# A transformer block in fp32: another order of the seven second products, two more steps in the second norm, a split of the row maxima on other engines, and a second store buffer

## The chip, the cores and the metric

The kernel runs on one core of a Trainium2 chip. A core has five engines that work side by side, each through its own instructions in order: TensorE (PE, matrix products; PEld is its weight load), VectorE (DVE), ScalarE (ACT), GpSimd (POOL) and SyncE (SP), which issues the DMAs here. They wait for each other by semaphores. The metric is device time in microseconds (us): the kernel before took 2392.91 us as the median of three runs (2387.88 to 2393.16).

## The reference

One transformer block on 2048 tokens of width 576, conditioned by a vector `c`:

```
mod = (silu(c) @ w_mod).reshape(c.shape[0], 6, 1, -1)
sa, ca, ga, sb, cb, gb = (mod[:, i] for i in range(6))
h = layernorm(x) * (1 + ca) + sa
x = x + ga * attention(h)           # 32 heads of width 18, one key and one value head for all
h = layernorm(x) * (1 + cb) + sb
x = x + gb * mlp(h)                 # layernorm again, 576 -> 4608, gelu (tanh form), 4608 -> 576
```

Scores of the attention are scaled by 18 ** -0.5 and go through a softmax over 2048 keys. All inputs and outputs are fp32.

## The kernel before, in words

**Split numbers.** Products of the large operands run in a format of fewer bits (F32R). An operand is therefore split into a high part (rounded by a copy into F32R) and a low part (the value minus the high part), and a product is three matmuls: high by high, high by low, low by high. Most of POOL's work, and some of ACT's and DVE's, is making such pairs.

**Stages.** A short stage makes the modulation, the first norm and the queries, keys and values. Then comes the attention, then the MLP, in two halves of 1024 tokens each.

**Attention.** 32 quads of four heads and 512 tokens (`NQT`), each with 16 steps `kc` of 128 keys. ACT takes the exponentials of the scores (L796). At the same time PE and DVE work on the next quad: for each query the maximum of its scores is found by L315 (products), L816 and L814 (reductions on DVE). `smax_fin2` (L351) closes this at `kc` 13: PE transposes the 16 columns of maxima, ACT copies the negative to `mf` (L356), POOL makes the high part `ms[:, 0]` (L357) and the low part (L358), and four DMAs (L362) write these rows into the next quad's operand `qst`; the scores of the next quad need them. Two lists are worked off beside that, in `between` (L818), a step at a time: `fill` (one step in every second `kc`) and `prep` (one step in most `kc`).

`fill` holds, from quad 8 on, the output projection of a finished block (`wo_block`) and then `ln2_block` (L566): the norms ahead of the MLP, tile by tile (`ln2_tile`, L519). For blocks 0 and 1 (`fine`) such a tile is: statistics of X in two steps (DVE bn_stats L140 and L144, then POOL L146 and L147); three POOL operations that make `h` (L536 to L538); one step later bn_stats of `h` on DVE (L140 again); and so on to the transposes. Eight such tiles fall into the attention, four from quad 8 and four from quad 16 on; the other eight (blocks 2 and 3) lie in the MLP's first half.

`prep` is `weight_parts` (L657): POOL multiplies the second MLP weight, forms sums of its quarters, splits each (L664 high, L665 low, into a buffer named `r2`) and SP stores it to DRAM (`w2scr`, `w2sum`, and for some groups of the first weight `w1scr`). There is one `r2` buffer, so a split waits until the store of the one ahead has left it.

**MLP.** 18 groups of 256 hidden columns (`NG`), for each of the two token halves: 36 steps `v`. The first product of a step is done in Strassen's way, in seven products (`product`, L1010, names A11, S2, S3, A12, S1, A22, S4, in this order, 6 or 8 matmuls of 512 columns each) on sums of quarters of the tokens that `op_pieces` (L877) makes. `gelu` (L1015) follows in three parts that are issued by calls of `g_()`: ACT (bias, square), then DVE and tanh on ACT, then the last product on DVE (L1032) with the split of the result into a unit (ACT L1034 high, POOL L1035 low).

The second product of a step `v` is issued in pieces of 12 matmuls of 288 columns by calls of `t_()`, one between each two products of step `v` + 1. In the first half it is plain (`fc2`, L1128). In the second half (`v` of 18 to 34) it is again seven products (`fc2s`, L1085), in the order of the table `SEVEN`: the operands are four quarters of the gelu's result (A11, A12, A22 are split as they are) and four sums (S1 to S4) that `sums` (L1062) makes on POOL (L1072 to L1082, with L1069 and L1070 for the split), issued step by step by calls of `s_()`. From the second such step on, the last of the seven pieces comes a step later, so that what PE runs in step `v` + 1 is: product A11, piece 7 of the step before; product S2, piece 1; product S3, piece 2; product A12, piece 3; product S1, piece 4; product A22, piece 5; product S4, piece 6. Gelu A12 of step `v` is the last to start, at product S4, and its third part is issued after product S2 of step `v` + 1. The pieces are gathered in two PSUM buffers (`psA`) and added to the result by DVE (L1103). Their seven weight buffers `W2S` are loaded anew from `w2scr` and `w2sum` by `load_w2s` (L1055) as soon as a piece is done.

## Time and profile before

| | |
|---|---|
| median of three runs | 2392.91 us |
| the profiled execution's own time | 2392.28 us |
| its span, first to last instruction | 2390.5 us |
| mean granted TensorE clock | 0.986 of full |
| PE busy | 2313.4 us (97%) |
| DVE busy | 1882.9 us (79%) |
| ACT busy | 1656.6 us (69%) |
| POOL busy | 1296.0 us (54%) |
| attention, roughly | 140 to 1450 us |
| MLP, first and second half, roughly | 1466 to 1930, 1930 to 2390 us |

A busy PE in this table is one with a matmul in flight, not one at its peak. In rows of the timeline the columns are start, duration of the group, engine, line, operation, tiles, shape and count, and in brackets the idle time of the engine before the row and what ended it. In rows of stretches the columns are the stretch, its length, the busy time of PE, PEld, DVE, ACT and POOL with their numbers of instructions, the granted clock, the DMA share and GB/s.

### The profile page before, as it was taken

Reading aid. Unit: us, or ns where it says so; the run is one execution under the profiler, and the core shown is the slowest. Engines: PE = TensorE matmul, PEld = TensorE weight load, DVE = VectorE, ACT = ScalarE, POOL = GpSimd, SP = SyncE. Lnnn points to the kernel's source line nnn. Section 1 sums busy time; section 2 is a strip of 40 time slices with the busy share of each in tenths; the row PEclk is TensorE's granted clock in tenths of the full one; section 3 lists DMA queues with packets and bytes.
Section 4 is the critical chain, followed back from the end, with each engine's and each line's share of the span. In section 5 each row is a group of like instructions: output and inputs, shape, how many; then the busy total and the mean of one; then the engine's idle time right before and its main releaser. Section 6 shows DMA issues by size and latency. Waiting matters only on the chain.

```text
span 2390.5 us, 44703 instructions
## 1 busy us (share of the span) xinstructions
PE 2313.4 (97%) x16382; PEld 1432.6 (60%) x16382; DVE 1882.9 (79%) x3330; ACT 1656.6 (69%) x3163; POOL 1296.0 (54%) x1552
## 2 busy tenths in 40 slices
PE   8999999999999999999999999999999999999998
PEld 6643444454434443434544336999999888888877
DVE  6589999979989879989799955666666767767766
ACT  5569999979989878989799996444444534333333
POOL 6501444436664346564434332688888656666666
PEclk9999999999999999999999999999999999999999
DMA  6412122221222112222122224334444465555553
GB/s 217 139 60 71 49 80 79 78 69 66 69 68 75 66 58 80 70 70 72 67 68 81 72 70 148 131 139 169 157 154 167 147 183 160 163 153 160 160 157 110
DMA packets 145627, 259.92 MB, mean 109 GB/s; under 512 B 15755, under 2 KB 56587, under 8 KB 145409
## 3 DMA queue, kind: packets, MB, share of 16 engines
q1 hardware_dynamic: 145409, 257.07, 33.7%
q8 instruction: 129, 2.11, 0.4%
q14 instruction: 89, 0.73, 0.1%
HBM read 156.11 MB, written 92.01 MB: 104 GB/s over the span
## 4 chain that ended last, share of the span: by engine, by line
PE 81%; POOL 6%; ACT 4%; DMA 3%; DVE 3%; issue 2%; SPq 1%; POOLq 0%; DVEq 0%; ACTq 0%
PE psC L783 19%; PE psB L1010 16%; PE psA L1128 9%; PE psB L794 9%; PE psM L315 9%; PE psA L1097 8%; PE psB L804 4%; PE psB L244 2%; ACT P L796 2%; PE psB L595 2%; POOL big L1035 1%; DMA w2scr<-r 1%; ACT big L1034 1%; DMA w2sum<-r 1%; POOL Z L536 1%
## 5 line engine op out<-in xcount | busy, mean ns | idle before, releaser
L796 ACT ACTIVATE P<-psB 128x512 f32<-128x512 f32 x2048 | 1049.9, 619 | 19.9 <-PE psB L794 17.2
L816 DVE TENSOR_REDUCE mx<-psM 128x1 f32<-128x512 f32 x1476 | 944.9, 683 | 61.2 <-PE psM L315 28.7
L783 PE MATMUL psC<-P,V 128*32 128x256 f32 (+1 forms) x6056 | 603.9, 470 | 12.6 <-ACT O L614 12.6
L315 PE MATMUL psM<-KS,qst 64*128 64x512 f32 x1722 | 600.0, 435 | 10.8 <-DVE mx L816 10.8
L794 PE MATMUL psB<-qst,KS 64*128 64x512 f32 x2048 | 602.9, 436 | 4.5 <-DMA qst<-ms 3.0
L794 PEld LDWEIGHTS psB<-qst,KS 64*128 64x128 f32 x2048 | 302.1, 185 | 173.2 <-issue 75.7
L1010 PE MATMUL psB<-ops,w1a 128*128 128x512 f32 x1512 | 400.9, 403 | 3.2 <-DVE gx L1032 2.5
L315 PEld LDWEIGHTS psM<-KS,qst 64*128 64x128 f32 x1722 | 286.8, 186 | 134.4 <-DVE mx L814 93.2
L1010 PEld LDWEIGHTS psB<-ops,w1a 128*128 128x128 f32 x1512 | 278.6, 193 | 53.6 <-DVE gx L1032 3.4
L783 PEld LDWEIGHTS psC<-P,V 128*32 128x32 f32 x6056 | 119.9, 108 | 235.8 <-issue 212.3
L1128 PE MATMUL psA<-w2s,big 128*128 128x288 f32 x1488 | 256.2, 296 | 0.0
L1128 PEld LDWEIGHTS psA<-w2s,big 128*128 128x128 f32 x1488 | 221.7, 188 | 6.7 <-POOL big L1035 0.2
L807 ACT ACTIVATE xc<-psB 128x512 f32<-128x512 f32 x246 | 148.8, 605 | 92.8 <-PE psM L315 71.4
L1103 DVE TENSOR_TENSOR XT<-psA,XT 128x576 f32<-128x576 f32 x170 | 125.2, 753 | 87.0 <-PE psA L1097 85.5
L1030 ACT ACTIVATE psB<-gs 128x512 f32<-128x512 f32 x144 | 86.7, 602 | 122.5 <-DVE gs L1029 122.5
L814 DVE CUSTOM_DVE_ANT_0 xc<-psM,xc 128x512 f32<-128x512 f32 x246 | 167.4, 680 | 3.3 <-PE psM L315 2.3
L1097 PE MATMUL psA<-w2s,big 128*128 128x288 f32 x816 | 131.2, 309 | 26.0 <-POOL big L1035 13.8
L1132 DVE TENSOR_TENSOR XT<-psA,XT 128x576 f32<-128x576 f32 x152 | 113.1, 748 | 47.3 <-PE psA L1128 47.1
L1097 PEld LDWEIGHTS psA<-w2s,big 128*128 128x128 f32 x816 | 119.9, 196 | 42.1 <-ACT big L1034 19.6
L1035 POOL TENSOR_TENSOR big<-gx,big 128x512 fp32r<-128x512 f32 x72 | 97.5, 1354 | 86.9 <-ACT big L1034 86.5
L804 PEld LDWEIGHTS psB<-KD,qst 64*128 64x128 f32 x246 | 45.3, 184 | 163.7 <-ACT P L796 112.6
L1034 ACT ACTIVATE big<-gx 128x512 fp32r<-128x512 f32 x72 | 45.6, 633 | 126.5 <-DVE gx L1032 126.5
(196 smaller groups left out, 3278.8 us busy)
## 6 DMA issues: line engine op xcount, KB each, us to landing
w1a<-w1scr SPq DMA_DIRECT2D x154, 256.0 KB
w1scr<-w1a SPq DMA_DIRECT2D x98, 256.0 KB
w2scr<-r SPq DMA_DIRECT2D x72, 288.0 KB
w2sum<-r SPq DMA_DIRECT2D x68, 288.0 KB
w2s<-w2sum SPq DMA_DIRECT2D x68, 288.0 KB
w2s<-w2scr SPq DMA_DIRECT2D x29, 576.0 KB
qst<-qscr SPq DMA_DIRECT2D x192, 72.0 KB
w2s<-w2scr SPq DMA_DIRECT2D x34, 288.0 KB
```

The costliest lines, as they stand in the source:

```text
L315: pe.matmul(o, QST[n][64 * g:64 * g + 64, p, 128 * qt:128 * (qt + 1)], KS[64 * g:64 * g + 64, 512 * kb:512 * (kb + 1)], start=True, stop=True)
L783: pe.matmul(PVt[n][32 * j:32 * (j + 1), cs], V[:, kc, :], t[:, j, cs], start=(kc == 0 and h0 == 0), stop=(kc == 15), skip_group_check=True)
L794: pe.matmul(t, KS[64 * g:64 * g + 64, 128 * kc:128 * (kc + 1)], QST[n][64 * g:64 * g + 64, i, :], start=True, stop=True)
L796: ac.activation(P[n, kc][:, 2 * i + g, :], t, AF.Exp, scale=SCALE)
L804: pe.matmul(t, QST[n][64 * g:64 * g + 64, p, 128 * qt:128 * (qt + 1)], KD1[64 * g:64 * g + 64, :], start=True, stop=True)
L807: ac.activation(XC[-1], t, AF.Relu)
L814: ve.tensor_tensor_reduce(c, t, c, 1.0, -3.0e38, ALU.add, ALU.max, o)
L816: ve.tensor_reduce(o, t, axis=AX.X, op=ALU.max)
L1010: pe.matmul(o, x, y, start=(first and i == 0), stop=(i == len(terms) - 1), skip_group_check=True)
L1097: pe.matmul(p[:, i, :288], x[:, ts_], W2S[k][:, y], start=(bool(first) and q == 0), stop=(q == 2), skip_group_check=True)
L1103: ve.tensor_tensor(o, p[:, :, :288], o, op=ALU.add)
L1128: pe.matmul(p[:, nn, :288], x, y, start=(q == 0), stop=(q == len(terms) - 1))
```

## The change

Five edits, which shift the lines below them by one or two:

1. The table `SEVEN` lists the pieces as S3, A22, A11, A12, S2, S1, S4 (before: A11, A12, S3, A22, S2, S1, S4), and `load_w2s` loads the weights in the same order. `sums` has one step less (S2's split goes with the two sums ahead of it), and its later steps are issued after products A11, S3 and A12 (before: after S2, S3, A12 and S1).
2. `ln2_tile` for blocks 0 and 1 has two steps more between `h` and its statistics.
3. `smax_fin2`: ACT writes the high part of the maxima straight from PSUM, DVE makes the low part from PSUM; POOL has no part in it any more; `ms` has one buffer, `mf` is gone.
4. `r2`, the buffer of the split weights ahead of their store, has two buffers and lies in another pool; `bst` has three buffers instead of four.
5. In `op_pieces` the low part of T4 goes to the engine `e2`, and for step 0 `e2` is POOL: POOL makes the low parts of T4 and B22 there, and of T4 at step 18.

```diff
     def smax_fin2(n):
         p = psB()
         pe.transpose(p[:16, :128], MR.pop(n), ident)
-        ms = pa.tile([16, 2, 128], F32R, name="ms", bufs=2)
-        mf = pa.tile([16, 128], F32, name="mf", bufs=2)
-        ac.activation(mf, p[:16, :128], AF.Copy, scale=-1.0)
-        po.tensor_copy(ms[:, 0], mf)
-        po.tensor_tensor(ms[:, 1], mf, ms[:, 0].bitcast(F32), op=ALU.subtract)
+        ms = pa.tile([16, 2, 128], F32R, name="ms")
+        ac.activation(ms[:, 0], p[:16, :128], AF.Copy, scale=-1.0)
+        ve.scalar_tensor_tensor(ms[:, 1], p[:16, :128], -1.0, ms[:, 0].bitcast(F32), op0=ALU.mult, op1=ALU.subtract)
...
         po.tensor_tensor(h, h, BC[:, 0, :], op=ALU.add)
         yield
-        if not fine:
+        yield
+        if fine:
             yield
         mv, rs = small()
         stt = ln_stats1(h)
...
-            o = px.tile(shape, F32R, name="r2")
+            o = pb.tile(shape, F32R, name="r2", bufs=2)
...
-              "T3": (10, 0, ve), "T4": (12, 2, ve), "t0": (0, 4, e2), "t1": (1, 9, e2)}
+              "T3": (10, 0, ve), "T4": (12, 2, e2), "t0": (0, 4, e2), "t1": (1, 9, e2)}
...
-    SEVEN = (("A11", 1, None), ("A12", 0, (0, 0)), ("S3", 1, (1, 1)), ("A22", 0, (1, 0)), ("S2", 1, None),
+    SEVEN = (("S3", 1, (1, 1)), ("A22", 0, (1, 0)), ("A11", 1, None), ("A12", 0, (0, 0)), ("S2", 1, None),
              ("S1", 1, (1, 1)), ("S4", 0, (0, 1)))
...
-        w = ("B11", "B21", "T3", "T4", "T2", "T1", "B22")[k]
+        w = ("T3", "T4", "B11", "B21", "T2", "T1", "B22")[k]
...
         po.tensor_tensor(s2, s1, h[0][0], op=ALU.subtract)
-        yield
         parts("S2", s2)
...
+    form = op_pieces(YR[0], po)
     b2_scaled(B2["b"])
...
         w_("A11")
         ac.activation(U[:, 0], ba, AF.Copy)
         g_()
+        s_()
...
         if v != 1:
             t_()
         g_()
-        s_()
         more("-B11 +T2", "-T4")
...
         gens.append(gelu(v, 1, 1, be))
         g_()
-        s_()
         more("-T3 -B21")
```

The places where instructions move. First PE in the middle of the MLP's second half, before: from product A11 of a step to its product A12 and the piece behind it. L1010 is a product, L1097 a piece of the second product; `big` holds the units of A12 and the sums, `gt` those of A11 and A22, and `w1a` the weight of piece 7.

```order
L1010 MATMUL psB<-ops,w1a 128x512 x6
L1097 MATMUL psA<-w1a,big 128x288 x12
L1010 MATMUL psB<-ops,w1a 128x512 x6
L1097 MATMUL psA<-w2s,gt_24668 128x288 x12
L1010 MATMUL psB<-ops,w1a 128x512 x6
L1097 MATMUL psA<-w2s,big 128x288 x12
L1010 MATMUL psB<-ops,w1a 128x512 x6
L1010 MATMUL psB<-opt,w1a 128x512 x2
L1097 MATMUL psA<-w2s,big 128x288 x12
```

And the same stretch of the changed kernel, where L1009 and L1095 are the same two lines:

```order
L1009 MATMUL psB<-ops,w1a 128x512 x6
L1095 MATMUL psA<-w1a,big 128x288 x12
L1009 MATMUL psB<-ops,w1a 128x512 x6
L1095 MATMUL psA<-w2s,big 128x288 x12
L1009 MATMUL psB<-ops,w1a 128x512 x6
L1095 MATMUL psA<-w2s,gt_24604 128x288 x12
L1009 MATMUL psB<-ops,w1a 128x512 x6
L1009 MATMUL psB<-opt,w1a 128x512 x2
L1095 MATMUL psA<-w2s,gt_24604 128x288 x12
```

Before, the piece behind product S2 reads A11 and the next one A12; now they are S3 and A22, then A11, and A12 comes one product later, behind S1.

POOL in the same part of the program, before, from the sum S3 at the end of a step to the split of S2 in the next. L1072 is S3, L1075 and L1076 are the two other sums, L1069 and L1070 a split, and L1035 the low part of A12:

```order
L1072 TENSOR_TENSOR yr<-yr 128x512
L1069 CAST big<-yr 128x512
L1070 TENSOR_TENSOR big<-yr,big 128x512
L1035 TENSOR_TENSOR big<-yr,big 128x512
L1075 TENSOR_TENSOR yr<-yr 128x512
L1076 TENSOR_TENSOR yr<-yr 128x512
L1069 CAST big<-yr 128x512
L1070 TENSOR_TENSOR big<-yr,big 128x512
```

The changed kernel there (each line number is one less):

```order
L1071 TENSOR_TENSOR yr<-yr 128x512
L1068 CAST big<-yr 128x512
L1069 TENSOR_TENSOR big<-yr,big 128x512
L1074 TENSOR_TENSOR yr<-yr 128x512
L1075 TENSOR_TENSOR yr<-yr 128x512
L1068 CAST big<-yr 128x512
L1069 TENSOR_TENSOR big<-yr,big 128x512
L1034 TENSOR_TENSOR big<-yr,big 128x512
```

S3 has kept its place; the low part of A12 now stands behind the two sums and the split of S2, four operations later.

DVE in the attention, in a quad without norm tiles, before; L348 and L349 close the maxima of a quad and the rows of L816 and L814 are the reductions of the quad after:

```order
L348 TENSOR_REDUCE mxf<-mx_4581 128x8
L349 TENSOR_REDUCE mxf<-mx_4581 128x8
L816 TENSOR_REDUCE mx_5158<-psM 128x1 x5
L814 ISA xc,mx_5158<-psM,xc 128x512
L814 ISA mx_5158 128x1
```

And in the changed kernel:

```order
L348 TENSOR_REDUCE mxf<-mx_4569 128x8
L349 TENSOR_REDUCE mxf<-mx_4569 128x8
L815 TENSOR_REDUCE mx_5144<-psM 128x1 x3
L356 SCALAR_TENSOR_TENSOR ms<-psB,ms 16x128
L815 TENSOR_REDUCE mx_5144<-psM 128x1 x2
L813 ISA xc,mx_5144<-psM,xc 128x512
L813 ISA mx_5144 128x1
```

The low part of the maxima now stands in DVE's order between the third and the fourth of these reductions.

## The prediction

> **What bounds the kernel now.** I read the page first, then the busy times by stretch, then the timeline where a stretch is slow. The span, and the two halves of the MLP by stretch:

> ```profile
> span 2390.5 us, 44703 instructions
> 1938.44:2353.07 414.63, 390.30 (x2145) 338.27 (x2145) 294.46 (x432) 154.22 (x256) 263.63 (x241) 0.96 0.56 158
> 1510.68:1854.00 343.32, 343.32 (x2066) 310.72 (x2065) 224.69 (x363) 155.30 (x271) 291.34 (x390) 1.00 0.45 157
> ```

> In the first half (second row) PE is busy for 343.32 of 343.32 us at a granted clock of 1.00: nothing to win there. In the second half it is busy for 390.30 of 414.63 at 0.96, so PE stands and is also clocked lower. One step of it, in the timeline:

> ```profile
> 2008.49 1.57 PE L1010 MATMUL psB<-ops,w1a 128*128 128x512 f32 x6
> 2009.90 1.75 PE L1097 MATMUL psA<-w2s,gt 128*128 128x288 f32 x12
> 2011.48 1.56 PE L1010 MATMUL psB<-ops,w1a 128*128 128x512 f32 x6
> 2012.36 0.68 DVE L1032 SCALAR_TENSOR_TENSOR yr<-psB,yr 128x512 f32<-128x512 f32 x1
> 2013.76 0.53 PE L1097 MATMUL psA<-w2s,big 128*128 128x288 f32 x2 [0.71 <-ACT big L1034]
> 2013.78 1.27 POOL L1035 TENSOR_TENSOR big<-yr,big 128x512 fp32r<-128x512 f32 x1 [4.21 <-ACT big L1034]
> 2015.10 2.55 PE L1097 MATMUL psA<-w2s,big 128*128 128x288 f32 x10 [0.81 <-POOL big L1035]
> 2017.45 2.19 PE L1010 MATMUL psB<-ops,w1a 128*128 128x512 f32 x6
> ```

> Piece 2 (A12, the row at 2013.76) needs the last gelu of the step before. DVE finishes that at 2013.04, ACT makes the high part and POOL the low part, and PE stands twice. Product S2 shows that six such matmuls take 2009.90 - 2008.49 = 1.41 us, so S3 is through at 2012.89 and 0.87 is lost until 2013.76. Twelve of a piece take 2011.48 - 2009.90 = 1.58, two of them 0.26, and from 2014.02 to 2015.10 another 1.08 is lost: 1.95 us together. Then the ten matmuls at 2015.10 take 2.35 instead of 1.32. The granted clock (the column ahead of the DMA share) of the two stretches behind the pauses:

> ```profile
> 2015.10:2017.45 2.35, 2.35 (x10) 2.35 (x11) 0.76 (x1) 0.00 (x0) 2.27 (x2) 0.56 0.16 60
> 2017.45:2019.95 2.50, 2.50 (x10) 1.98 (x10) 0.76 (x1) 0.00 (x0) 2.36 (x4) 0.73 0.30 69
> ```

> So the pauses cost more than their length in this step. They recur in 17 steps (first row, from the list of waits: total, times, longest). The other rows show the same place in the first, the third and the last of these: twice ten matmuls in 1.58 or 1.59 at full clock, once in 2.58:

> ```profile
> PE psA L1097 <- ACT big L1034: 12.1, 17, 0.8
> 1938.44 1.58 PE L1097 MATMUL psA<-w2s,big 128*128 128x288 f32 x10 [0.81 <-POOL big L1035]
> 1990.08 1.59 PE L1097 MATMUL psA<-w2s,big 128*128 128x288 f32 x10 [0.82 <-POOL big L1035]
> 2353.07 2.58 PE L1097 MATMUL psA<-w2s,big 128*128 128x288 f32 x10 [0.81 <-POOL big L1035]
> ```

> The attention is bound otherwise, and differs by quad. Stretches from one copy of the maxima to the next: a quad without norm, one with a norm tile that runs well, and the five long quads:

> ```profile
> 373.70:412.03 38.33, 37.87 (x323) 15.45 (x323) 36.47 (x70) 37.70 (x76) 17.93 (x25) 1.00 0.23 75
> 711.25:750.40 39.15, 38.67 (x328) 15.94 (x328) 36.70 (x71) 38.07 (x77) 17.93 (x25) 1.00 0.22 74
> 583.05:624.97 41.92, 40.30 (x327) 16.55 (x328) 37.99 (x76) 38.38 (x78) 27.82 (x33) 0.96 0.19 62
> 664.01:711.25 47.24, 42.62 (x328) 16.99 (x327) 38.39 (x77) 38.57 (x78) 27.88 (x33) 0.93 0.20 67
> 881.84:924.74 42.90, 40.29 (x328) 16.20 (x328) 37.98 (x76) 38.06 (x77) 28.61 (x35) 0.96 0.21 67
> 924.74:966.86 42.12, 40.14 (x326) 16.36 (x327) 37.98 (x76) 38.36 (x78) 26.61 (x31) 0.96 0.23 75
> 1005.93:1051.60 45.67, 42.01 (x328) 16.87 (x328) 38.24 (x77) 38.28 (x78) 23.91 (x29) 0.93 0.22 70
> ```

> ACT is busy for 37.70 of 38.33 in the plain quad: it sets the pace, DVE (36.47) is close. In the long quads all engines' work is nearly the same and the quad is longer, so somebody waits. The waits of the whole run, and rows from the longest quad:

> ```profile
> POOL r L664 <- DMA w2scr<-r: 118.9, 48, 6.1
> DVE bst L140 <- POOL Z L538: 20.7, 13, 3.7
> 664.01 0.27 ACT L356 ACTIVATE mf<-psB 16x128 f32<-16x128 f32 x1
> 667.94 0.28 POOL L357 CAST ms<-mf 16x128 fp32r<-16x128 f32 x1
> 672.40 0.59 PE L794 MATMUL psB<-qst,KS 64*128 64x512 f32 x2 [2.45 <-DMA qst<-ms]
> 690.80 2.31 POOL L536 TENSOR_SCALAR Z<-XT,mv,rs 128x576 f32<-128x576 f32 x1
> 694.69 1.41 POOL L538 TENSOR_TENSOR Z<-Z,BC 128x576 f32<-128x576 f32 x1
> 696.13 0.46 DVE L140 BATCH_NORM_STATS2 bst<-Z 128x6 f32<-128x288 f32 x1 [2.60 <-POOL Z L538]
> ```

> POOL, held up by stores from its one buffer, comes to the maxima 3.7 us after ACT made `mf` (664.28), and the scores wait for the DMA; later DVE stands 2.60 for `h`, and with it the maxima, PE and ACT.

> **The change part by part.** *Order of the pieces.* No matmul is added or removed; A12 is piece 4 now, behind product S1. PE reaches it later by two pieces (1.58 each) and two products of eight matmuls (8 x 1.41 / 6 = 1.88 each): 6.9 us, so at 2019.8 instead of 2012.89. Its low part moves behind four POOL operations, which are two sums and a split like these three:

> ```profile
> 2006.22 1.30 POOL L1072 TENSOR_TENSOR yr<-yr 128x512 f32<-128x512 f32 x1 [1.28 <-DVE yr L1032]
> 2007.58 0.61 POOL L1069 CAST big<-yr 128x512 fp32r<-128x512 f32 x1
> 2008.27 1.29 POOL L1070 TENSOR_TENSOR big<-yr,big 128x512 fp32r<-128x512 f32 x1
> 2009.67 1.74 PEld L1097 LDWEIGHTS psA<-w2s,gt 128*128 128x128 f32 x12
> ```

> The four take 1.30 + 1.30 + 0.61 + 1.29 = 4.5 us from 2009.56 on and fill POOL's 4.21 of idle time, so A12's low part ends at 2015.3, hardly later than now (2015.05), 4.4 ahead of its use. What is late next? Piece 1, now S3, whose sum and split are the three rows themselves. The high part is there at 2008.19 and the first weight load of piece 1 at 2009.67; the low part is there at 2009.56 and needed by the third matmul, two of 0.13 later, at about 2009.93. The margin is about 0.4 us: small, but the chain ahead of S3 (gelu A21 behind product A22) keeps its place, and PE is at full speed there already, so nothing shortens it. A step at full clock is 2015.10 - 1990.08 = 25.02 us; without the pauses 23.07. The 16 steps between the rows of 1938.44 and 2353.07 take 414.63: 414.63 - 16 x 23.07 = 45.5. The pause ahead of 1938.44 is another 1.95, and the lower clock behind 2353.07, as at 2015.10, 1.03 + 0.62 (2.50 against 1.88 for product A12). Together **-49**, of which 17 x 1.95 = 33 is standing and 16 lower clock. If A12 were no earlier, or S3 as late as A12, it would be 0; I take -49, since the margins come from rows.

> [...]

> *Two steps more, second store buffer.* The three POOL operations for `h` take 690.80 to 696.10, 5.3 us, more than the one step of two `kc` (38.33 / 8 = 4.8 us) that they had, so `h` was late wherever POOL was not idle. With three steps it is 14.4, and the stores (longest wait 6.1) need no waiting any more, or less. The added steps cost nothing by themselves: block 0 takes 8 + 44 calls of `fill` instead of 8 + 36, and 64 lie between two blocks. If all five long quads come down to 39.15, this is 41.92 + 47.24 + 42.90 + 42.12 + 45.67 - 5 x 39.15 = 24.1. If POOL stays late by other waits it is nothing. I take **-22**.

> *The maxima.* POOL's two operations leave, and with them the 2.45 above (counted there). DVE gets 32 small operations that must wait for ACT's copy; behind each stand the next reductions, for which PE waits. Rows of a plain quad:

> ```profile
> 412.03 0.27 ACT L356 ACTIVATE mf<-psB 16x128 f32<-16x128 f32 x1
> 412.49 0.69 DVE L816 TENSOR_REDUCE mx<-psM 128x1 f32<-128x512 f32 x1 [0.24 <-PE psM L315]
> 669.40 0.28 DVE L164 COPY yr<-psB 128x128 f32<-128x128 f32 x1
> ```

> DVE is idle from 412.25 to 412.49, ACT's copy is done at 412.30, and the nearest DVE operation, a copy of 128 columns from PSUM, takes 0.28. So a quad's reductions start about 0.1 later, and DVE has 38.33 - 36.47 = 1.9 per quad to make it up. Bounds: -1 (the DMA starts earlier) to 32 x 0.28 = 9; I take **+1**.

> *POOL at steps 0 and 18, `bst`.* POOL has 20 idle us ahead of its first split of a gelu in step 0, so the two low parts cost nothing there:

> ```profile
> 1480.79 1.29 POOL L1035 TENSOR_TENSOR big<-gx,big 128x512 fp32r<-128x512 f32 x1 [20.17 <-ACT big L1034]
> ```

> At step 18 T4 is needed five products later. `bst` turns on one engine in order. **0** together, -1 to +2.

> **The sum.** The profiled execution took 2392.28, that is its span and 1.8 around it; the median of the runs is 0.6 more. 2392.28 - 49 - 22 + 1 = 2322.3: **2322**.

> **The rivals.** *S3 is the new wait.* If POOL ends S3 later than now by L, PE stands L less 0.4 in 16 or 17 steps, and the clock may fall again. At L = 0.8 it is 17 x 0.4 + 16 = 23, so 2345; if it is as late as A12 was, the whole 49 is back: 2371. For it: the smallest margin here. Against: nothing ahead of S3 on POOL has changed. 10%.

> *The norm stays late.* POOL still waits for loads or for the second store; the 22 shrinks to nothing: 2344. For it: POOL has 28 of 42 us of work in these quads. Against: 14.4 us for 5.3 of work. 10%.

> *The clock stays lower.* If the steps' pattern and not the pauses lowers it, the 16 stay: 2338. For it: only 0.96 in this half, and not every pause is followed by it. Against: 0.56 directly behind a pause, 1.00 in the first half. 4%. [...]

> *DVE waits for ACT in each quad: slower.* If ACT had eight exponentials (37.70 / 76 = 0.5 us each) ahead of the copy, DVE, and behind it PE, would stand up to 4 us in 31 quads: 31 x 4 = 124, so 2446. It decides from 71 / 31 = 2.3 us per quad on. Against: ACT takes the copy at 412.03, with the next reduction's matmul not yet through. 3%.

> *The order does not do what it says* (a piece still tied to the last gelu by a shared buffer) while something else costs a few us: within 0.3% of before. 2%.

> **How the numbers follow.** The forecast has 71%, 2312 to 2332: the bounds of the small terms, and 2 for the norm either way. The range goes to the two middle rivals, 2308 to 2347; left out above are S3 fully late, DVE's waits and no change. A difference under 0.3%, about 7 us, can't be told from none. Faster 0.95, same 0.02, slower 0.03.

> **What would show it.** Right: steps of 23.1 us in the second half at a clock of 1.00, no wait of PE for L1034 or L1035's successors; quads with norm at 39 us, no DVE wait for `h`; no POOL wait for stores. Wrong: a wait of PE ahead of piece 1, a clock below 1 without pauses, quads over 41 us, or DVE idle ahead of its low part of the maxima.

## The result, and the profile after

| | before | after |
|---|---|---|
| median of the runs (lowest to highest) | 2390.53 us (2387.88 to 2393.16) | 2320.74 us (2319.79 to 2321.38) |
| profiled execution, its span | 2392.28, 2390.5 us | 2319.79, 2318.0 us |
| from the start to product A11 of step 19, ahead of the first of the 17 pauses before | 1930.29 us | 1906.85 us (-23.4) |
| from there to the end | 460.21 us | 411.15 us (-49.1) |
| first to last copy of the maxima (32 quads) | 1281.35 us | 1259.14 us (-22.2) |

The ratio is 0.9708, with an interval of 0.9691 to 0.9725: 2.9% faster, 1.3 us below the time that was forecast (2322). One of the four runs of one experiment, with the maxima back on POOL, came in a slower state (2656.57 us) and is left out of its median.

The busy times by stretch of the kernel after: the span, a stretch of the second half of the MLP, and the first half (columns as before: length, busy time of PE, weight loads, DVE, ACT and POOL, granted clock, DMA share, GB/s).

```profile
span 2318.0 us, 44793 instructions
1900.00:2310.00 410.00, 408.41 (x2392) 363.85 (x2391) 323.13 (x474) 169.01 (x281) 292.74 (x264) 1.00 0.60 173
1510.00:1854.00 344.00, 344.00 (x2073) 311.34 (x2073) 224.59 (x363) 155.91 (x271) 288.76 (x388) 1.00 0.45 157
```

The second half has become like the first: PE is busy for 408.41 of 410.00 us and the clock is 1.00, where it was 390.30 of 414.63 at 0.96. One step of it in the timeline after (the lines of products and pieces are L1009 and L1095 now, the split of a sum L1068 and L1069, the low part of a gelu L1034):

```profile
1977.27 1.30 POOL L1069 TENSOR_TENSOR big<-yr,big 128x512 fp32r<-128x512 f32 x1
1977.54 1.56 PE L1009 MATMUL psB<-ops,w1a 128*128 128x512 f32 x6
1978.70 1.74 PEld L1095 LDWEIGHTS psA<-w2s,big 128*128 128x128 f32 x12
1978.94 1.75 PE L1095 MATMUL psA<-w2s,big 128*128 128x288 f32 x12
...
1983.21 1.29 POOL L1034 TENSOR_TENSOR big<-yr,big 128x512 fp32r<-128x512 f32 x1
...
1988.86 1.76 PE L1095 MATMUL psA<-w2s,big 128*128 128x288 f32 x12
```

The row at 1978.94 is S3, the first piece now; its low part ends at 1977.27 + 1.30 = 1978.57, in time. The row at 1988.86 is A12, whose low part (1983.21) ends at 1984.50, 4.4 us ahead. All twelve matmuls of each stand in one row without a bracket: PE doesn't stand. Nor is either wait of PE for the units of a piece left in the list of waits.

The five long quads of the attention, and a plain one, in stretches from copy to copy of the maxima:

```profile
580.55:620.18 39.63, 39.16 (x328) 16.16 (x326) 37.75 (x76) 38.14 (x77) 21.17 (x26) 1.00 0.20 65
659.69:699.28 39.59, 39.14 (x328) 16.19 (x329) 37.44 (x75) 37.95 (x78) 20.89 (x26) 1.00 0.25 80
870.51:909.80 39.29, 38.85 (x323) 15.95 (x324) 37.74 (x76) 37.61 (x77) 27.72 (x33) 1.00 0.23 73
909.80:949.44 39.64, 39.17 (x328) 16.17 (x326) 37.76 (x76) 38.12 (x77) 21.19 (x24) 1.00 0.25 80
988.97:1028.52 39.55, 39.08 (x328) 16.17 (x328) 37.44 (x75) 37.94 (x77) 20.92 (x26) 1.00 0.25 80
371.67:410.04 38.37, 37.92 (x323) 15.40 (x323) 36.66 (x71) 37.68 (x76) 13.73 (x19) 1.00 0.24 75
```

Together they are 219.86 - 197.70 = 22.2 shorter, and the clock is 1.00 in all five. The quad behind each block's long ones takes 0.8 more now (38.33 before, 39.13 and 39.17 after). The plain quad takes 38.37 against 38.33, so DVE's new operation costs nothing there, though DVE is busy for 36.66 instead of 36.47. That operation and ACT's copy in the timeline after:

```profile
659.69 0.27 ACT L355 ACTIVATE ms<-psB 16x128 fp32r<-16x128 f32 x1
659.99 0.28 DVE L356 SCALAR_TENSOR_TENSOR ms<-psB,ms 16x128 fp32r<-16x128 f32 x1
```

The low part of the maxima starts 0.03 us after ACT's copy ends; in the quad before that began at 664.01, POOL came to it 3.7 us later. From the list of waits after:

```profile
POOL r L663 <- DMA w2scr<-r: 42.2, 14, 10.8
POOL r L663 <- DMA w2sum<-r: 27.7, 10, 10.9
```

The two rows were 118.9 and 82.6 us before: POOL's wait for the stores is less, but not gone. DVE's wait for `h` is 7.9 us in 8 waits where it was 20.7 in 13. The five waits in the attention (12.8 us) are gone; the eight of the MLP's first half have stayed as they were.

### The profile page after: what moved, and what is told of

Read it like the earlier page. It is cut to its first block, busy times and chain, and to the rows that moved or that the text cites. A ratio compares the mean times of both kernels' runs of the same rounds, so it can differ in the third digit from the quotient of the medians.

```text
span 2318.0 us, 44793 instructions
## 1 busy us (share of the span) xinstructions
PE 2280.2 (98%) x16382; PEld 1417.4 (61%) x16382; DVE 1883.3 (81%) x3359; ACT 1654.0 (71%) x3163; POOL 1277.0 (55%) x1491
## 4 chain that ended last, share of the span: by engine, by line
PE 86%; ACT 4%; POOL 2%; DVE 2%; issue 1%; DMA 0%; SPq 0%; POOLq 0%; DVEq 0%; ACTq 0%
PE psC L782 22%; PE psB L1009 16%; PE psB L793 12%; PE psM L315 10%; PE psA L1126 9%; PE psA L1095 8%; PE psB L803 4%; PE psB L594 2%; ACT P L795 2%; ACT O L613 1%; PE psA L594 1%; PE psB L152 0%; PE psB L244 0%; PE psB L199 0%; ACT xc L806 0%
## 5 line engine op out<-in xcount | busy, mean ns | idle before, releaser
L315 PE MATMUL psM<-KS,qst 64*128 64x512 f32 x1722 | 595.8, 431 | 0.2
L1009 PE MATMUL psB<-ops,w1a 128*128 128x512 f32 x1512 | 391.3, 396 | 3.2 <-DVE gx L1031 2.6
L315 PEld LDWEIGHTS psM<-KS,qst 64*128 64x128 f32 x1722 | 284.1, 184 | 123.4 <-DVE mx L813 89.8
L1009 PEld LDWEIGHTS psB<-ops,w1a 128*128 128x128 f32 x1512 | 271.5, 188 | 52.0 <-DVE gx L1031 3.5
L1126 PE MATMUL psA<-w2s,big 128*128 128x288 f32 x1488 | 255.4, 295 | 0.0
L1126 PEld LDWEIGHTS psA<-w2s,big 128*128 128x128 f32 x1488 | 221.3, 188 | 6.6
L132 POOL MEMSET qst<- 32x1024 f32 x62 | 58.6, 945 | 197.9 <-PE psM L315 93.1
L1034 POOL TENSOR_TENSOR big<-gx,big 128x512 fp32r<-128x512 f32 x72 | 96.3, 1338 | 68.8 <-ACT big L1033 68.4
L803 PE MATMUL psB<-KD,qst 64*128 64x512 f32 x246 | 121.9, 495 | 0.0
```

Of the source, the lines that this page charges most:

```text
L315: pe.matmul(o, QST[n][64 * g:64 * g + 64, p, 128 * qt:128 * (qt + 1)], KS[64 * g:64 * g + 64, 512 * kb:512 * (kb + 1)], start=True, stop=True)
L803: pe.matmul(t, QST[n][64 * g:64 * g + 64, p, 128 * qt:128 * (qt + 1)], KD1[64 * g:64 * g + 64, :], start=True, stop=True)
L1009: pe.matmul(o, x, y, start=(first and i == 0), stop=(i == len(terms) - 1), skip_group_check=True)
L1126: pe.matmul(p[:, nn, :288], x, y, start=(q == 0), stop=(q == len(terms) - 1))
```

## The experiments

Times are medians. The kernel before, run beside them on three chips, had 2389.03, 2388.28 and 2391.54 us.

**The two halves of the change.** One kernel is the one before with the new order of pieces alone (`SEVEN`, the loads of the weights, the steps of `sums`); the other is the one after with the old order:

```diff
-    SEVEN = (("A11", 1, None), ("A12", 0, (0, 0)), ("S3", 1, (1, 1)), ("A22", 0, (1, 0)), ("S2", 1, None),
+    SEVEN = (("S3", 1, (1, 1)), ("A22", 0, (1, 0)), ("A11", 1, None), ("A12", 0, (0, 0)), ("S2", 1, None),
```

> The kernel before with the new order of the seven pieces and of the sums alone. Theory (the pauses ahead of A12 and the lower clock behind them are one cost, 49 us, and have nothing to do with the attention): 2391 - 49 = 2342, steps of 23.1 us and a clock of 1.00 in the second half. Rival (the lower clock has another cause that the attention edits took away): only the standing goes, 2391 - 33 = 2358, clock still under 1 in the second half.

> The changed kernel with the old order of pieces and sums; all else as changed. Theory (the parts add): 2321 + 49 = 2370, the second half again with steps of 25.9 us on average, the attention as short as in the changed kernel (last copy of the maxima at 1392). Rival (the low parts that moved to GpSimd in the MLP, or the moved buffers, matter too): off from 2370 by more than 3 us.

The order alone took 2339.26 us, ratio 0.9792 (0.9776 to 0.9809): -49.8. The rest alone took 2367.2, ratio 0.9913 (0.9899 to 0.9928): -21.8. Both theories hold, the second narrowly: 2367.2 is 2.8 below 2370, and its rival began at 3. 49.8 + 21.8 = 71.6 is close to the 69.8 of the whole: the halves hardly touch each other.

**The parts of the rest.** All of these have the new order. Without the two added steps:

```diff
-        yield
-        yield
-        if fine:
-            yield
+        yield
+        if not fine:
+            yield
```

> The changed kernel without the two added steps in the norm; two store buffers and the split of the maxima stay. Theory (three GpSimd operations of 5.3 us do not fit in one step of 4.8, whatever the stores do): VectorE waits again for h, 1 to 2 us in each of eight tiles, 2321 + 8 to 15 = 2329 to 2336. Rival (the stores alone held GpSimd up): it stays at 2321 to 2324 and no norm quad is over 40 us.

With one buffer for the stores (the two other tiles that share this buffer have `bufs=1` too):

```diff
-            o = pb.tile(shape, F32R, name="r2", bufs=2)
+            o = pb.tile(shape, F32R, name="r2", bufs=1)
```

> The changed kernel with one store buffer instead of two; the two added steps and the split of the maxima stay. Theory (14.4 us for 5.3 of work are enough for a store of 6 us as well): 2321 to 2324, norm quads at 39.5 us as in the changed kernel, GpSimd waits for stores again, for 100 to 250 us in all, and nobody waits for GpSimd. Rival (the stores are what made h late): 2330 to 2340, with VectorE waiting for h.

With neither:

> The kernel after without the two added steps and with one buffer for the stores: of the change, the order of the pieces and the maxima on VectorE are left. Taken alone, the two edits undone cost 6.5 us (steps) and 3.0 us (buffers). Theory (each covers most of what the other cures, so together they are worth the whole term of the norm, and the maxima bring nothing): 2337 to 2342 us, as the run with the order alone (2339.3). Rival (the three edits are independent, the rest of the norm's gain is that of the maxima, which no longer hold up GpSimd): 2328 to 2333 us.

With one buffer for the stores and the maxima split by POOL (the added steps stay):

```diff
-        ms = pa.tile([16, 2, 128], F32R, name="ms")
-        ac.activation(ms[:, 0], p[:16, :128], AF.Copy, scale=-1.0)
-        ve.scalar_tensor_tensor(ms[:, 1], p[:16, :128], -1.0, ms[:, 0].bitcast(F32), op0=ALU.mult, op1=ALU.subtract)
+        ms = pa.tile([16, 2, 128], F32R, name="ms", bufs=2)
+        mf = pa.tile([16, 128], F32, name="mf", bufs=2)
+        ac.activation(mf, p[:16, :128], AF.Copy, scale=-1.0)
+        po.tensor_copy(ms[:, 0], mf)
+        po.tensor_tensor(ms[:, 1], mf, ms[:, 0].bitcast(F32), op=ALU.subtract)
```

> The kernel after with the maxima split by GpSimd again (three buffers' room goes back to them, so the stores have one buffer, as in the run with one buffer for the stores, 2323.7 us, which is what this one is compared with). In the profile of the kernel before GpSimd stands 214.6 us in 31 waits at L357 for ScalarE's maxima. Theory (that standing has slack: the added steps of the norm cover it): 2323 to 2328 us, the quads of the two middle blocks at 39 to 40 us but for one or two of about 42. Rival (what lies behind the maxima on GpSimd's queue, the splits of the weights and the norm's multiplications, comes late again): at least two quads per block of 42 us or more, 2330 to 2340 us.

| new order, and | us | ratio (interval) | first to last copy |
|---|---|---|---|
| nothing else | 2339.26 | 0.9792 (0.9776 to 0.9809) | 1278.52 |
| maxima | 2333.18 | 0.9769 (0.9754 to 0.9783) | 1271.88 |
| maxima, two store buffers | 2327.26 | 0.9743 (0.9728 to 0.9757) | 1267.77 |
| steps | 2328.45 | 0.9746 (0.9730 to 0.9762) | 1266.88 |
| maxima, steps | 2323.73 | 0.9728 (0.9713 to 0.9742) | 1260.99 |
| all | 2320.74 | 0.9708 (0.9691 to 0.9725) | 1259.14 |

In all rows but the first, `bst`, T4 and the pool of `r2` are as after. The last column is from the traces.

By the medians the steps are worth 6.5 us beside two store buffers and 9.5 beside one; the second buffer is worth 3.0 beside the steps and 5.9 without; the maxima are worth 6.1 without the steps and 4.7 beside them. The rows come from more than one chip. By the ratios, each against the kernel before on its own chip, the six are 8.4 and 9.8, 4.8 and 6.2, 5.5 and 4.3. So each is known to about 2 us, and that steps and buffer cover part of each other's work (2.9 us by the medians, 1.4 by the ratios) is not shown. Of the 6.1 of the maxima, 1.6 us lie behind the attention, where the maxima have no part: from the last copy to the first product A11 it is 52.59 us with nothing else, 50.96 with the maxima, and 51.17 with the maxima on POOL again.

The steps alone (6.5) came out between theory and rival. The buffer came out at its theory's time, but not in every mark: one quad with norm takes 42.49 us (below), and PE does wait for POOL there. My theory that the maxima bring nothing fell, 2333.18 lying at the edge of the rival's range; beside the steps, 2328.45 is just above the theory's range and below the rival's.

What the maxima do on POOL is in the trace of the kernel that has them there again, where one quad takes 43.93 us at a clock of 0.96. (Another, from 913.57, takes 44.28; there PE waits 2.09 us for POOL's `Z`, as it does with the maxima on DVE in the quad of 42.49 below, but here the clock falls behind that wait. So this one is not the maxima.) The quad as a stretch, and rows from its start:

```profile
658.66:702.59 43.93, 41.33 (x328) 16.72 (x328) 37.41 (x74) 38.32 (x77) 23.95 (x29) 0.96 0.22 72
```

```profile
658.66 0.27 ACT L356 ACTIVATE mf<-psB 16x128 f32<-16x128 f32 x1
659.08 1.43 POOL L537 TENSOR_TENSOR Z<-Z,BC 128x576 f32<-128x576 f32 x1
660.59 1.42 POOL L538 TENSOR_TENSOR Z<-Z,BC 128x576 f32<-128x576 f32 x1
661.96 0.28 POOL L357 CAST ms<-mf 16x128 fp32r<-16x128 f32 x1
666.42 0.59 PE L795 MATMUL psB<-qst,KS 64*128 64x512 f32 x2 [2.54 <-DMA qst<-ms]
```

ACT's copy ends at 658.93; on POOL the operations of `h` are queued ahead, so the split starts 3.0 us later, and PE stands 2.54 for the DMA behind it. It is the wait that stood in the longest quad before (2.45), this time behind the norm's own work and not behind a store. With the maxima on DVE and one store buffer the same quad reads:

```profile
657.99:697.53 39.54, 39.07 (x328) 16.18 (x328) 37.42 (x75) 37.93 (x77) 25.33 (x30) 1.00 0.25 80
```

That kernel also shows what POOL's waits for stores are worth. From its list of waits, then one quad as a stretch, and a row of the timeline in it:

```profile
POOL r L663 <- DMA w2scr<-r: 158.0, 50, 13.3
POOL r L663 <- DMA w2sum<-r: 115.9, 37, 13.4
```

```profile
908.25:950.74 42.49, 39.40 (x328) 16.43 (x329) 37.74 (x76) 38.12 (x78) 27.45 (x31) 1.00 0.25 81
```

```profile
910.88 0.66 PE L152 MATMUL psB<-ident,Z 128*128 128x128 f32 x4 [2.67 <-POOL Z L549]
```

158.0 + 115.9 = 274 us of waiting against 70 with two buffers, and 3.0 us of time (4.8 by the ratios): of the quads, only the one at 908.25 is longer than with two buffers by more than 0.2, because PE waits once for POOL's `Z`. Without the added steps, but with two buffers, the norm is late in two quads per block, and the later one of them again has a lower clock:

```profile
581.16:622.46 41.30, 39.70 (x326) 16.46 (x326) 38.03 (x77) 38.28 (x77) 28.75 (x35) 1.00 0.19 62
661.67:704.22 42.55, 40.78 (x328) 16.46 (x328) 38.48 (x78) 38.19 (x78) 25.78 (x30) 0.96 0.23 74
```

**The margin of S3, and the pauses.** Four kernels are the one after with work on POOL put ahead of S3's sum, in each step of the second half: a copy (0.61 us), a subtraction (1.3), both, and two subtractions. The one with 1.3:

```diff
+        po.tensor_tensor(s1, h[0][0], h[1][0], op=ALU.subtract)
         po.tensor_tensor(s3, h[0][0], h[1][0], op=ALU.subtract)
         parts("S3", s3)
```

> The kernel after with a copy of 128x512 on GpSimd (0.61 us) ahead of S3's sum in each of the steps of the second half; the output stays that of the reference. Theory (margin about 0.4 us): PE waits 0.2 to 0.3 us in 16 or 17 steps, 2323 to 2327 us, the clock unchanged. Rival 1 (margin over 0.6 us): 2320 to 2322 us. Rival 2 (even so short a wait lowers the clock): 2330 to 2345 us.

> The kernel after with one more subtraction of 128x512 on GpSimd ahead of S3's sum in each of the steps of the second half (1.3 us; its result is overwritten, the output stays that of the reference). The prediction put the margin of S3 at about 0.4 us. Theory (margin 0.4 us, and a standing PE lowers the granted clock behind it, as in the kernel before): PE waits 0.8 to 1.0 us for L1069 or L1070 in 16 or 17 steps, 14 to 16 us, and up to 16 us more through the clock: 2334 to 2352 us; the granted clock falls below 0.9 behind the waits. Rival 1 (margin over 1.3 us): 2320 to 2322 us. Rival 2 (the wait comes, the clock stays 1.00, since one pause of under 1 us in 23 is too little for the gate): 2333 to 2338 us with PEclk all 9s.

> The kernel after with a copy and a subtraction of 128x512 on GpSimd ahead of S3's sum in each step of the second half (1.9 us; results overwritten, the output stays that of the reference). With 1.3 us PE stood 0.42 to 0.50 us in 16 steps and the granted clock stayed 1.00, so the margin is about 0.8 us. Theory (PE stands 1.1 us per step, in one pause of that length or two shorter ones; pauses of this length do lower the granted clock, as in the kernel before): 17 x 1.1 = 19 us of standing and 8 to 16 us of clock: 2347 to 2356 us, with a granted clock under 0.98 in the second half. Rival (a pause of 1.1 us in 24 lowers nothing; in the kernel before it took 1.95 us): 2337 to 2342 us at a clock of 1.00.

> The kernel after with two subtractions of 128x512 on GpSimd ahead of S3's sum in each step of the second half (2.6 us; results overwritten, the output stays that of the reference). S3's high part is then late too, so PE should stand twice ahead of one piece, about 0.8 us before its first matmul and about 1 us before its third: the pattern of the kernel before, at another piece. Theory (the pauses themselves lower the granted clock): 17 x 1.8 = 31 us of standing and about 16 of clock, 2361 to 2372 us, the clock of the second half 0.96 to 0.97. Rival (the lower clock of the kernel before belonged to its order of pieces and not to the pauses): 2348 to 2354 us at a clock of 1.00.

| put ahead of S3 | us | ratio (interval) | step | clock of the half |
|---|---|---|---|---|
| 0 | 2320.74 | 0.9708 (0.9691 to 0.9725) | 23.08 | 1.00 |
| 0.61 | 2319.59 | 0.9709 (0.9694 to 0.9723) | 23.11 | 1.00 |
| 1.3 | 2330.05 | 0.9756 (0.9739 to 0.9772) | 23.79 | 1.00 |
| 1.9 | 2341.92 | 0.9802 (0.9788 to 0.9817) | 24.46 | 1.00 |
| 2.6 | 2370.34 | 0.9916 (0.9899 to 0.9932) | 25.14 or 26.7 | 0.96 |

The step is the distance between equal rows of the timeline. Steps are 0.71, 1.38 and 2.06 us longer for 1.3, 1.9 and 2.6 us of work, so S3's margin is 0.5 to 0.6 us. With 0.61 no wait of PE is seen: the first rival. With 1.3 the wait comes, but less of it than my theory had, and the clock doesn't move: 2330.05 lies between the two rivals, nearer to the second. With 1.9 the rival holds: 1.38 us of standing in each of 17 steps, 23 us, and a clock of 1.00. With 2.6 the theory holds, in the pattern of the kernel before. A step of the kernel with 1.9, the pause in the timeline and the step as a stretch:

```profile
1983.44 1.60 PE L1097 MATMUL psA<-w2s,big 128*128 128x288 f32 x10 [0.81 <-POOL big L1069]
```

```profile
1983.44:2007.90 24.46, 23.58 (x134) 20.41 (x134) 18.40 (x27) 9.64 (x16) 18.33 (x18) 1.00 0.59 169
```

The same of the kernel with 2.6: two pauses, then the two stretches behind them, a step at full clock and one with the clock lowered:

```profile
1987.40 0.54 PE L1097 MATMUL psA<-w2s,big 128*128 128x288 f32 x2 [0.70 <-POOL big L1068]
1988.75 1.92 PE L1097 MATMUL psA<-w2s,big 128*128 128x288 f32 x10 [0.81 <-POOL big L1069]
```

```profile
1988.75:1990.46 1.71, 1.71 (x10) 1.71 (x11) 0.76 (x1) 0.00 (x0) 1.63 (x2) 0.81 0.18 65
1990.46:1993.02 2.56, 2.56 (x7) 1.98 (x7) 1.36 (x2) 0.63 (x1) 2.42 (x3) 0.50 0.41 114
1911.79:1936.93 25.14, 23.59 (x134) 20.42 (x134) 18.39 (x27) 9.63 (x16) 19.00 (x18) 1.00 0.67 200
1962.07:1988.75 26.68, 25.16 (x135) 21.80 (x135) 18.41 (x27) 9.63 (x16) 18.99 (x18) 0.94 0.54 155
```

The pauses of 0.70 and 0.81 are those of the kernel before (0.71 and 0.81), at another piece and for another engine's work. By the durations of the ten matmuls behind the second pause, the clock is lowered in 10 of 17 steps here, and in 10 of 17 of the kernel before. So the lower clock belongs to the pauses and not to the order (what sets the 10 of the kernel before apart is in the last section): 17 x 2.06 = 35 us of standing and 10 x 1.54 = 15 of clock are 50, and 2370.34 - 2320.74 = 49.6 was measured.

## Why the prediction was right

**The order, -49.** Right in sum and in both parts: -49.1 in the trace from the second half on, -49.8 for the order alone, -46.5 on top of the rest (-49.0 by the ratios). The steps are 23.08 (forecast 23.07) and the clock is 1.00. The experiment with 2.6 us gives the same 50 back by the same pauses, so the split into 33 of standing and 16 of clock is shown, not only worked out. What would be late next was named rightly, S3, and its margin (0.4) only a little too small.

**The clock.** With 1.38 us of standing in each step (1.9 us of work) the clock of the half was 1.00; with 1.95 (the kernel before) or 2.06 (2.6 us of work), in two pauses close together, it was lowered in 10 of 17 steps, for a loss of 1.54 to 1.6 in each. The rival that the lower clock would stay is refuted.

**Norm and maxima, -22 and +1.** Right in sum: the quads give -22.2, and the rest alone -21.8. That it is right to 0.2 us is in part luck: the five quads came down to 39.54 on average and not to the 39.15 of the text's bound of 24.1, and the text gives no reason for the 2 us that it takes off that bound. The shares were not worked out. The text names the wait for the maxima as one that goes with POOL's two operations, but counts it in the norm's term; the runs show 4 to 6 us for the maxima leaving POOL's queue, 6.5 to 10 for the steps and 3 to 6 for the buffer. The term of +1 for DVE was mis-sized on the safe side: the plain quad is longer by 0.04 us, within what plain quads differ by. The mark "no POOL wait for stores" was wrong: 70 us of it are left, though no quad with norm is over 39.7 us with them.

**POOL at steps 0 and 18, `bst`, 0.** Right: no PE wait there. From the last copy of the maxima to the first product A11 the kernel after takes 50.98 against 52.60 us. These 1.6 were in no term. Most of it is in DVE operations on the way to the last of the output projection. They ran beside two POOL operations on the biases before and run alone after. One of them (rows below) is 0.95 shorter, the two behind it take 2.35 instead of 2.82, and PE's two short waits for that chain (0.32 and 0.52) are gone:

```profile
1456.03 2.52 POOL L568 TENSOR_TENSOR b2g<-b2g,BC 128x576 f32<-128x576 f32 x1 [9.81 <-DMA b2g<-in_b]
1457.45 1.64 DVE L622 TENSOR_TENSOR T<-T,R 128x512 f32<-128x512 f32 x1
```

```profile
1435.36 0.69 DVE L621 TENSOR_TENSOR T<-T,R 128x512 f32<-128x512 f32 x1
```

**The sum.** The two terms that were off, +1 for DVE and nothing for the 1.6, miss in the same direction and don't cancel. 2392.28 - 49.1 - 22.2 - 1.6 and 0.3 for the first copy of the maxima, which comes later, are 2319.7; the profiled execution took 2319.79.

**The rivals.** None came true. That S3 becomes the wait is a real danger all the same: with S3 as late as A12 was, the text gave 2371, and 2.6 us of work ahead of it gave 2370.34.

## What to carry to other kernels

Where an engine stands twice for the high and the low part of the same late operand, move another piece ahead of it whose operands are made earlier, and price the gain as standing plus the lower clock where the profile shows one behind it; here the clock was a third of it (16 of 49 us). A total of waits is no price: with one store buffer POOL waited 204 us more, and of the quads one was longer, by 2.85 us; one small operation of 0.28 us, queued behind long work, made one quad longer by 4.4 (43.93 against 39.54), because PE stood at the end of its chain. Whether two edits that help the same engine cover part of each other's gain has to be measured with runs of each alone and of both on the same chip; here the overlap stayed within what the runs scatter.

## What the runs showed of the hardware

The clock's fall did not go by the length of a pause alone. In the attention, one of 2.54 us (kernel with the maxima on POOL) was followed by a clock of 0.68, and one of 2.67 (kernel with one store buffer, at 910.88) by 1.00. The stretches behind the two, in that order:

```profile
666.00:669.00 3.00, 2.58 (x15) 1.04 (x15) 0.70 (x2) 1.20 (x3) 1.04 (x2) 0.68 0.28 98
```

```profile
911.00:914.00 3.00, 3.00 (x30) 1.56 (x30) 1.97 (x5) 2.42 (x6) 2.85 (x5) 1.00 0.02 4
```

Why the two differ is not shown. In the second half of the kernel before, the clock is 0.50 for 3.41 us at a time, and these stretches (from 1964.19, 2015.39, 2042.70 and so on) start at whole multiples of 3.413 us from each other: the first two are 51.20 us apart, 15 x 3.413, the first and the third 78.51, 23 x 3.413. With this half divided into stretches of that length from 1964.19 on and back, two pairs of neighbours, in which the first holds the pauses of a step:

```profile
1960.78:1964.19 3.41, 1.89 (x10) 1.21 (x9) 1.31 (x3) 0.63 (x1) 2.06 (x2) 1.00 0.60 172
1964.19:1967.60 3.41, 3.41 (x13) 2.92 (x12) 1.52 (x2) 0.00 (x0) 3.19 (x4) 0.50 0.13 14
1988.08:1991.49 3.41, 1.94 (x12) 1.71 (x13) 1.24 (x2) 0.60 (x1) 2.66 (x3) 1.00 0.55 162
1991.49:1994.91 3.42, 3.42 (x22) 3.05 (x21) 1.48 (x3) 1.24 (x2) 3.27 (x4) 1.00 0.44 98
```

```profile
598.85:602.27 3.42, 1.99 (x20) 0.93 (x17) 2.52 (x6) 2.29 (x5) 3.34 (x5) 1.00 0.01 4
602.27:605.68 3.41, 3.41 (x16) 1.08 (x14) 3.30 (x7) 2.09 (x4) 2.44 (x4) 0.50 0.24 85
1486.32:1489.73 3.41, 1.67 (x6) 1.05 (x6) 1.45 (x4) 2.43 (x5) 1.12 (x1) 1.00 0.90 333
1489.73:1493.15 3.42, 2.92 (x16) 2.56 (x17) 2.54 (x4) 2.35 (x5) 0.76 (x2) 1.00 0.47 129
```

What decides there stays open.

The DVE operation at 1457.45 took 1.64 us beside POOL's (2.52 us from 1456.03), and 0.69 at 1435.36 in the kernel after, where POOL is idle. Neither waits for the other's data, and why it took longer was not tested by itself.
